# Score products in row-half tile order, and new engine orders, in a four-layer attention and GLU kernel

## The chip, the cores and the metric

The kernel runs on one core of a Trainium2 chip. The metric is the device time of one execution in microseconds (us). The time before is 384.71 us, the median of three runs (384.37 to 385.68).

## The reference

The input `x` has 2048 tokens of 448 values in bf16. It goes through four layers; each layer normalizes its rows (mean and variance) and adds its result to `x`:

```python
x = x + _A_ref(_layernorm(x), wqkv, wo)
x = x + _B_ref(_layernorm(x), w_gate, w_up, w_down)
x = x + _A_ref(_layernorm(x), wqkv, wo)
x = x + _B_ref(_layernorm(x), w_gate, w_up, w_down)
```

`_A_ref` is attention with 16 heads of 28 values. Token s looks at 8 tokens only: s, s-2, s-4, ... s-14. Its logits are scaled, the missing tokens at the start are masked, a softmax follows, then the sum of the values and the product with `wo`. `_B_ref` is `(x @ w_gate) * (x @ w_up) @ w_down` with an inner width of 1792. Both attention layers share their weights, and so do both GLU layers.

## The kernel before, in words

Layers 0 and 2 are attention, layers 1 and 3 are the GLU. Tokens are put in two halves, even and odd ones, so that the window of 8 tokens at distance 2 becomes 8 neighbours. `x_sb` holds 16 blocks of 128 tokens. Each layer goes in chunks of 256 or 512 tokens (`ACH`, `BCH`, `SEQ`); chunks of neighbouring layers run beside each other.

**The long products.** TensorE does nearly all of its work in a mode where the array is split in two row halves of 64 rows and 128 columns (`MAIN = "R64"`). Two products, one per half, run at once: a *pair*. Queries and keys (`qk_chunk`), values (`v_group`), the gate and up products (`b_chunk`), the down product and the product with `wo` (`y_blocks`, both by `twin_blocks`) are all such pairs, issued through `whole` in the helper `pair` (profile line 347). A pair streams 256, 336, 448 or 512 columns.

**The short products.** Attention itself works on query blocks of 120 tokens (`qb_info`), two at a time. `attn_front` makes the scores: 32 products per query block, each with a key tile of 64 rows by 32 columns and some 64 to 80 query columns (line 831, mode `BURST = "C32"`). In the first eleven query blocks of layer 0 (`WIDE_S`) the tiles are 64 by 64 and there are 16 per block (mode C64). ScalarE takes the exponential (line 841), VectorE applies the mask (848), and `attn_back` multiplies with the values: 32 products per query block, on tiles of 64 by 32 (line 866). The result is copied out (880), its two parts are added (884), and `norm` divides by the sum (894 to 907). Their tiles sit at eight positions of the array: two row halves by four column strips. Which position follows which in time is set by the list comprehension on line 826 for scores and on line 859 for values. For values the column strip is the inner index: four strips of one row half, then four of the other. For scores before the change the row half `p` is the inner index: it alternates with every product.

**Bursts.** Short products and long products need different modes, so a run of short products stands between long ones as a *burst*. A burst can also be *merged*: some pairs of a long product next to it (its host) are then issued as eight products of 32 columns each, one per tile position (`strip`, line 350), in the same mode as the short ones, and the short products are put between these *sets of strips* in portions of eight. A set of strips does the work of one pair.

**The order of the work.** Every operation is an `Op` with its dependencies. The order on each engine is written out in the table `ORDER` (line 101), and the PSUM banks of each product in `BANKS` (163); `schedule` and `emit` only turn them into waits. An entry `A+B*H/k/f` in TensorE's list is a merged burst: the first f pairs of host H as they are, then the short products of A and B with k sets of strips of H between them, then the rest of H. Copies from PSUM (`QK` line 708, `V` line 800, `Oc` line 880, the transposes' 623) may be on ScalarE or VectorE; the lists say which. SyncE's list holds the loads, the transposing DMAs of the normalized rows (line 602) and the stores.

**The GLU's chain.** Rows of `x` after an attention layer are added by VectorE (924), get their statistics (578, 580) and are normalized (599), all on VectorE with two small steps on ScalarE; a transposing DMA then brings them to `xnTb`, and only then can the gate products of that chunk begin.

Of the kernel before, what the change touches and what calls it, by code (L numbers as in the profile page):

```python
# [93 lines left out]
def grp_nc(g):  # L94
# [22 lines left out]
    ),  # L117
    "act": (
# [12 lines left out]
    ),  # L131
    "dve": (
# [18 lines left out]
    ),  # L151
    "pool": (
        "21 24 39 28 23 18 29 35 40 25 36 26 20 32 44 33 37 19 27 22 41 34 38 42 30 65 43 31 63"
# [222 lines left out]
def build(nc, A_x, A_wqkv, A_wo, B_w_gate, B_w_up, B_w_down, out):  # L376
# [433 lines left out]
    def attn_front(li, g, prio):  # L810
        qbs, nc = grp_qbs(g), grp_nc(g)
        nd = len(qbs)
# [11 lines left out]
        KN = 64 if wide else 32  # L824
# [281 lines left out]
```

## Time and profile before

| | us |
|---|---|
| median of three runs | 384.71 |
| the profiled execution | 384.78 |
| its span (first to last instruction) | 382.8 |
| TensorE busy | 377.2 |
| VectorE busy | 288.7 |
| ScalarE busy | 197.2 |

The span is what the trace shows; the 1.98 us between it and the execution's time lie around it. A row of the timeline reads: start, length from the first start to the last end, engine, line, operation, tiles, shape, and the number of instructions that were merged into the row. The end of a product is modelled, so the start of the next row is the better mark. A row of the windows names a stretch and then each engine's busy time in it with the number of its instructions.

### The profile page before, as it was taken

What the parts mean: (1) busy time and instruction counts of PE and PEld (TensorE: products, weight loads), DVE (VectorE), ACT (ScalarE), POOL (GpSimd) and SP (SyncE); (2) the same over time, 40 slices, a digit from 0 to 9 for tenths busy, and PEclk for the clock granted to TensorE, in tenths of its full rate; (3) what the DMA queues carried; (4) which work ended last, traced back from release to release, by engine and by line L of the source; (5) the groups of instructions that cost most, each with busy time, mean ns of one, the idle gap of its engine ahead of it and who ended that gap; (6) DMA issues with size and microseconds to landing.
All of it is one profiled execution on the core that took longest, in us unless ns stands there. A gap on an engine that the chain in (4) does not pass through costs nothing.

```text
span 382.8 us, 14279 instructions
## 1 busy us (share of the span) xinstructions
PE 377.2 (99%) x6338; PEld 210.8 (55%) x6338; DVE 288.7 (75%) x652; ACT 197.2 (52%) x383; POOL 7.1 (2%) x33
## 2 busy tenths in 40 slices
PE   8999999999999999999999999999999999999997
PEld 3655577544454545446766666555555444445665
DVE  7998999998756876897567888668899687174443
ACT  4897887566426356156456236448653534125220
POOL 6000000000000000000000000000000000000000
PEclk9999999999999999999999999999999999999999
DMA  7665542700421030232001214320124002313004
GB/s 251 171 161 135 122 116 65 105 3 2 81 39 39 11 56 19 50 62 47 6 15 38 50 29 76 73 36 8 35 46 75 2 3 60 64 23 38 2 2 134
DMA packets 54880, 22.49 MB, mean 59 GB/s; under 512 B 45012, under 2 KB 54820, under 8 KB 54820
## 3 DMA queue, kind: packets, MB, share of 16 engines
q1 hardware_dynamic: 54676, 21.53, 26.5%
q8 instruction: 50, 0.82, 0.9%
q14 instruction: 10, 0.08, 0.1%
q10 hardware_dynamic: 144, 0.06, 0.1%
HBM read 8.54 MB, written 2.71 MB: 29 GB/s over the span
## 4 chain that ended last, share of the span: by engine, by line
PE 89%; DVE 6%; DMA 1%; ACT 1%; issue 1%; SPq 0%; DVEq 0%
PE ps L347 81%; PE ps L350 3%; PE ps L831 2%; PE ps L866 2%; PE ps L975 1%; DVE st L578 1%; DMA xnTb<-xn_sb 1%; DVE xn_sb L599 1%; DVE E_sb L848 1%; DVE x_sb L924 1%; DMA x_sb<-in_A_x_dram 1%; DVE oT L907 0%; PE ps L613 0%; DVE hT L963 0%; DVE R_sb L894 0%
## 5 line engine op out<-in xcount | busy, mean ns | idle before, releaser
L347 PE MATMUL ps<-xnTb,WGU 64*128 64x512 bf16 (+1 forms) x1900 | 173.7, 332 | 0.3
L347 PEld LDWEIGHTS ps<-xnTb,WGU 64*128 64x128 bf16 x1900 | 92.4, 94 | 71.5 <-ACT g_sb L960 1.5
L960 ACT ACTIVATE g_sb<-ps 128x512 bf16<-128x512 f32 (+1 forms) x140 | 69.0, 509 | 112.4 <-PE ps L347 93.8
L963 DVE TENSOR_TENSOR hT<-g_sb,ps 128x512 bf16<-128x512 bf16 (+1 forms) x140 | 77.7, 573 | 43.2 <-ACT g_sb L960 41.8
L347 PE MATMUL ps<-WD,hT 64*128 64x448 bf16 x802 | 83.5, 349 | 0.1
L347 PEld LDWEIGHTS ps<-WD,hT 64*128 64x128 bf16 x802 | 38.5, 94 | 33.4 <-DVE hT L963 0.5
L347 PE MATMUL ps<-xnTa,WQK 64*128 64x512 bf16 (+1 forms) x486 | 52.7, 352 | 0.6 <-issue 0.3
L924 DVE TENSOR_TENSOR x_sb<-x_sb,ps 128x448 bf16<-128x448 bf16 x62 | 36.8, 611 | 18.2 <-PE ps L347 18.1
L841 ACT ACTIVATE E_sb<-ps,shift_sb 128x1024 bf16<-128x1024 f32 (+1 forms) x36 | 37.5, 1068 | 11.6 <-PE ps L831 11.4
L578 DVE BATCH_NORM_STATS2 st<-x_sb 128x6 f32<-128x448 bf16 x64 | 38.5, 615 | 1.5 <-DMA x_sb<-in_A_x_dram 1.3
L599 DVE TENSOR_SCALAR xn_sb<-x_sb,mv,rstd 128x512 bf16<-128x512 bf16 (+1 forms) x64 | 35.1, 567 | 4.7 <-ACT rstd L583 4.5
L347 PEld LDWEIGHTS ps<-xnTa,WQK 64*128 64x128 bf16 x486 | 23.4, 94 | 18.4 <-issue 0.4
L708 ACT ACTIVATE qk<-ps 128x1024 bf16<-128x1024 f32 (+1 forms) x28 | 25.7, 929 | 8.7 <-PE ps L347 6.1
L347 PE MATMUL ps<-wo_g,oT 64*128 64x448 bf16 x256 | 29.5, 350 | 0.1
L895 ACT ACTIVATE R_sb<-R_sb 128x480 f32<-128x480 f32 (+1 forms) x34 | 19.9, 601 | 15.7 <-DVE R_sb L894 15.6
L848 DVE TENSOR_TENSOR E_sb<-E_sb,MK 128x1024 bf16<-128x1024 bf16 (+1 forms) x36 | 23.1, 656 | 5.2 <-ACT E_sb L841 5.2
L907 DVE TENSOR_TENSOR oT<-O_sb,R_sb 128x480 bf16<-128x480 f32 (+3 forms) x36 | 21.8, 624 | 6.5 <-ACT R_sb L896 6.5
L347 PE MATMUL ps<-WV,xnTa 64*128 64x336 bf16 (+3 forms) x252 | 23.3, 304 | 0.0
L894 DVE STREAM_SHUFFLE R_sb<-O_sb 128x480 f32<-128x480 f32 (+1 forms) x34 | 22.8, 691 | 0.0
L896 ACT ACTIVATE R_sb<-R_sb 128x480 f32<-128x480 f32 (+1 forms) x34 | 19.9, 599 | 0.2
L347 PEld LDWEIGHTS ps<-wo_g,oT 64*128 64x128 bf16 x256 | 12.1, 94 | 11.1 <-DVE oT L907 0.7
L866 PEld LDWEIGHTS ps<-E_sb,v_sb 64*32 64x32 bf16 x1088 | 12.6, 90 | 8.2 <-issue 3.6
(61 smaller groups left out, 215.4 us busy)
## 6 DMA issues: line engine op xcount, KB each, us to landing
out_dram<-x_sb SPq DMA_DIRECT2D x15, 112.0 KB, 1.8
x_sb<-in_A_x_dram SPq DMA_DIRECT2D x3, 448.0 KB, 5.7
hT<-in_A_wqkv_dram SPq DMA_DIRECT2D x4, 224.0 KB, 4.8
WGU<-in_B_w_gate_dram SPq DMA_DIRECT2D x4, 224.0 KB, 4.0
WGU<-in_B_w_up_dram SPq DMA_DIRECT2D x4, 224.0 KB, 4.4
WD<-in_B_w_down_dram SPq DMA_DIRECT2D x2, 448.0 KB, 4.9
WGU<-in_B_w_gate_dram SPq DMA_DIRECT2D x2, 336.0 KB, 4.6
WGU<-in_B_w_up_dram SPq DMA_DIRECT2D x2, 336.0 KB, 4.4
```

The costliest lines, as they stand in the source:

```text
L347: return lambda E: E.matmul(out(), lhs(), rhs(), start=start, stop=stop)
L578: sc.add("dve", one(lambda E, B=B: E.bn_stats(st6[:, B, :], x_sb[:, B, :]), ("bn", li, B)), 525.0, deps=[("x", li - 1, B)] + ([("xn", li - ...
L599: sc.add("dve", one(lambda E, B=B, dst=dst, src=src: E.tensor_scalar(dst, src, mv[:, B, 0:1], rstd[:, B:B + 1], ALU.subtract, ALU.mult), ( ...
L708: return E.activation(dst, src, ACT.Copy) if hasattr(E, "activation") else E.tensor_copy(dst, src)
L841: return E.activation(E_sb[:, slot, 2 * hp:2 * hp + 2, 0:w], ps[:, b0:b0 + 2, 0:w], ACT.Exp, bias=shift_sb[:, 0:1], scale=SCALE)
L848: return E.tensor_tensor(e, e, MK[:, kind, 0:nc].unsqueeze(1).unsqueeze(1).to_broadcast([128, 2, w // nc, nc]), ALU.min)
L866: parts[eb // 2].append((lambda E, b=b, c=c, o=o, vw=vw, eb=eb, eo=eo: E.matmul(ps[32 * b:32 * b + 32, bk[c], o:o + nc], vw, E_sb[64 * c:6 ...
L894: sc.add("dve", one(lambda E: E.stream_shuffle(R_sb[:, rs, 0:w], O_sb[:, os_, 0:w], [DH] * 32), ("Rs", li, qb)), dve_est(w) + 20.0, deps=[ ...
L907: return E.tensor_tensor(oT[:, :, a % HALF:a % HALF + z - a], O[:, :, a - tok:z - tok], R_sb[:, rs, 0:w].rearrange("p (h n) -> p h n", h=4 ...
L924: sc.add("dve", one(lambda E: E.tensor_tensor(x_sb[:, B, :], x_sb[:, B, :], ps[:, bk[w], 0:D], ALU.add), ("x", li, B)), dve_est(D), deps=[ ...
L960: sc.add("act", one(lambda E, gs=gs, bk=bk: E.activation(g_sb[:, gs, 0:nt], ps[:, bk[0], 0:nt], ACT.Copy), ("G", li, j, fc)), act_est(nt), ...
L963: sc.add("dve", one(lambda E, gs=gs, bk=bk, fc=fc: E.tensor_tensor(hT[:, fc, hs, 0:nt], g_sb[:, gs, 0:nt], ps[:, bk[1], 0:nt], ALU.mult), ...
```

## The change

One line of the code changes, that of the scores' order, and the tables `ORDER` and `BANKS` are new from end to end.

```diff
-        for hc, d, c, s_, p in [(hc, d, c, s_, p) for hc in range(4) for d in range(nd) for c in range(2) for s_ in range(64 // KN) for p in range(2)]:
+        for hc, d, p, c, s_ in [(hc, d, p, c, s_) for hc in range(4) for d in range(nd) for p in range(2) for c in range(2) for s_ in range(64 // KN)]:
```

The scores now go through four column strips of one row half and then through four of the other, as the values and the strips do. Of the tables, these entries of TensorE's list show the kind of difference (two of the list's pieces, in order):

```diff
-525 530 347 542 531 543 350 602 351 603 560*352/1/6 353 428
+542+560+543*353/6/1 428 602 429 603
...
-1325 1204 1326 1205 1365+1347+1348*1258/7 1261 1267 1278 1366 1270 1279 1335 1280 1371+1372*1271/7 1336
+1365*1204/1/3 1366*1205/1 1267 1325 1278 1326 1279 1270 1271 1280 1281 1347+1348+1371+1372*1272/7 1273 1335
```

Here 560, 1365 and 1366 are scores of one query block each; 542, 543, 1347, 1348, 1371 and 1372 are values. Counted through both lists, the bursts are:

| kind of burst | before | after |
|---|---|---|
| 32 short products of 32-column tiles, alone (one of those before has one set of strips) | 20 | 7 |
| 64 of them, without strips | 1 | 3 |
| 64 of them, one set of strips | 0 | 1 |
| 64 of them, two sets | 7 (6 scores, 1 values) | 14 (7 scores, 5 values, 2 mixed) |
| 64 of them, three to seven sets | 7 (all values) | 0 |
| 96 of them | 1 (seven sets) | 2 (five and six sets) |
| 128 of them | 1 (five sets) | 2 (seven sets each) |
| 16 products of 64-column tiles, alone | 4 | 2 |
| 32 of them, together | 3 | 4 |
| the first scores of layer 0 | 1 | 1 |

TensorE's list has 6338 products before and 6314 after, since 58 sets of strips become 54. VectorE's list grows from 595 to 600 entries and ScalarE's shrinks from 383 to 378: 19 copies move from ScalarE to VectorE and 14 the other way. In SyncE's list the four transposing DMAs of layer 1's second chunk stand at places 63, 64, 67 and 68 before, and at 61, 63, 64 and 65 after. At the start, all of the warming products stand before the first long product; at the end the order of the last three down products is 448, 224, 224 columns before and 224, 448, 224 after, the last of them the same.

128 rows, old and new, of tables (BANKS, ORDER) are left out of this document.

## The prediction

> **What bounds the kernel now.** I read the page's busy times first, then the windows, then the timeline of TensorE alone.
>
> ```profile
> PE 377.2 (99%) x6338; PEld 210.8 (55%) x6338; DVE 288.7 (75%) x652; ACT 197.2 (52%) x383; POOL 7.1 (2%) x33
> ```
>
> TensorE (PE) is busy for 377.2 of 382.8 us. A busy TensorE is not one at its peak, so the question is what stands in that time beside long products. The windows say who else is near its limit:
>
> ```profile
> 50.00:100.00 50.00, 49.78 (x984) 28.27 (x980) 47.04 (x109) 35.16 (x73) 0.00 (x0) 1.00 0.31 60
> 100.00:150.00 50.00, 50.00 (x848) 25.10 (x846) 34.41 (x73) 23.77 (x43) 0.00 (x0) 1.00 0.23 41
> ```
>
> The third busy time is VectorE's (DVE). From 50 to 100 us it has 47.04 of 50 us, so both engines bind there; from 100 us on it has 34.41, and TensorE alone sets the pace. The granted clock is 1.00. So a microsecond that leaves TensorE's list is worth a microsecond after 100 us and perhaps half of one before.
>
> What the long products cost when nothing disturbs them, from their own rows:
>
> ```profile
> 369.13 2.46 PE L347 MATMUL ps<-xnTb,WGU 64*128 64x256 bf16 x42
> 371.42 1.49 PE L347 MATMUL ps<-WD,hT 64*128 64x448 bf16 x14
> 372.75 0.93 PE L347 MATMUL ps<-xnTb,WGU 64*128 64x256 bf16 x14
> ```
>
> Start to start, 21 pairs of 256 columns take 2.29 us, 0.109 a pair; seven pairs of 448 take 1.33, 0.190 a pair. Now the burst's price can be read. It is the start of the next long row, less the start of the long row before plus that row's pairs, less one pair for each set of strips, since a set does a pair's work.
>
> ```profile
> 198.66 1.30 PE L347 MATMUL ps<-WD,hT 64*128 64x448 bf16 x12
> 199.89 0.32 PE L866 MATMUL ps<-E_sb,v_sb 64*32 64x64 bf16 x32
> 200.14 0.94 PE L347 MATMUL ps<-xnTb,WGU 64*128 64x256 bf16 x14
> 201.01 0.34 PE L866 MATMUL ps<-E_sb,v_sb 64*32 64x64 bf16 x32
> 201.28 1.12 PE L347 MATMUL ps<-WD,hT 64*128 64x448 bf16 x10
> 202.33 0.29 PE L831 MATMUL ps<-Qz,qk 64*32 64x64 bf16 x24
> ...
> 203.17 0.74 PE L347 MATMUL ps<-WD,hT 64*128 64x448 bf16 x6
> ```
>
> A lone burst of 32: 198.66 + 6 x 0.190 = 199.80, and the next long row starts at 200.14: 0.34 us. The one after: 200.14 + 7 x 0.109 = 200.90, against 201.28: 0.38. I use 0.36. A merged burst of 64 scores with two sets: 201.28 + 5 x 0.190 = 202.23, next 203.17, less two pairs: 0.56, where two lone bursts would be 0.72. Changing over and back is most of a lone burst, and that is what merging saves.
>
> **The change part by part.** I count the bursts in both lists (the table above) and price each kind. The other prices come from these rows:
>
> ```profile
> 276.33 0.92 PE L347 MATMUL ps<-wo_g,oT 64*128 64x448 bf16 x8
> ...
> 279.36 3.20 PE L347 MATMUL ps<-xnTb,WGU 64*128 64x512 bf16 x28
> 282.38 1.50 PE L347 MATMUL ps<-WD,hT 64*128 64x448 bf16 x14
> 283.83 0.59 PE L831 MATMUL ps<-Qz,qk 64*32 64x64 bf16 x32
> 284.35 0.93 PE L347 MATMUL ps<-WD,hT 64*128 64x448 bf16 x8
> ```
>
> A pair of 512 columns is (282.38 - 279.36)/14 = 0.216. The 96 short products with seven sets that stand in the gap: 276.33 + 0.76 = 277.09 to 279.36 is 2.27, less 7 x 0.216: 0.76. The lone scores at 283.83 should cost 0.36, but 282.38 + 1.33 = 283.71 to 284.35 is 0.64: 0.28 of it is a stall.
>
> ```profile
> 252.15 0.92 PE L347 MATMUL ps<-WD,hT 64*128 64x448 bf16 x8
> ...
> 254.94 1.12 PE L347 MATMUL ps<-WD,hT 64*128 64x448 bf16 x10
> ```
>
> 128 short products with five sets: 252.91 to 254.94 is 2.03, less 5 x 0.190: 1.08.
>
> ```profile
> 287.81 1.11 PE L347 MATMUL ps<-WD,hT 64*128 64x448 bf16 x10
> ...
> 290.54 0.74 PE L347 MATMUL ps<-WV,xnTa 64*128 64x336 bf16 x8
> ```
>
> 64 values with seven sets: 288.76 to 290.54 is 1.78, less 1.33: 0.45. Thirty-two more short products thus cost 0.09 over a lone burst, if enough sets stand between them.
>
> ```profile
> 42.90 0.92 PE L347 MATMUL ps<-WV,xnTa 64*128 64x448 bf16 x8
> 43.75 0.71 PE L866 MATMUL ps<-E_sb,v_sb 64*32 64x64 bf16 x64
> 44.40 0.61 PE L347 MATMUL ps<-xnTa,WQK 64*128 64x256 bf16 x8
> 44.94 0.80 PE L831 MATMUL ps<-Qz,qk 64*64 64x128 bf16 x32
> 45.92 0.50 PE L347 MATMUL ps<-xnTa,WQK 64*128 64x256 bf16 x6 [0.18 <-DVE qk L708]
> ```
>
> 64 without strips: 43.66 to 44.40, 0.74, as much as two lone bursts, so joining alone gains nothing. The scores of 64 by 64 tiles behind it: 44.84 to 45.92, 1.08, with a wait for VectorE's copy in it.
>
> ```profile
> 36.55 0.93 PE L347 MATMUL ps<-wo_g,oT 64*128 64x448 bf16 x8
> 37.41 0.42 PE L831 MATMUL ps<-Qz,qk 64*64 64x128 bf16 x16
> 37.76 0.93 PE L347 MATMUL ps<-wo_g,oT 64*128 64x448 bf16 x8
> ```
>
> ```profile
> 58.48 0.72 PE L347 MATMUL ps<-xnTb,WGU 64*128 64x256 bf16 x10
> 59.13 0.64 PE L831 MATMUL ps<-Qz,qk 64*64 64x128 bf16 x32
> 59.71 1.70 PE L347 MATMUL ps<-xnTb,WGU 64*128 64x256 bf16 x28
> ```
>
> Sixteen of them alone: 37.31 to 37.76, 0.45. Thirty-two together, undisturbed: 59.03 to 59.71, 0.68.
>
> Before: 20 x 0.36 = 7.20; 0.74; seven with two sets, 3.92; seven with more sets at 0.48 (between 0.45 and 0.56, nearer the first), 3.36; 0.76; 1.08; 4 x 0.45 = 1.80; 3 x 0.68 = 2.04. Sum 20.90.
>
> After: 7 x 0.36 = 2.52; 3 x 0.74 = 2.22; the one with one set 0.65 (between 0.56 and 0.74); seven scores with two sets 3.92, seven others at 0.52 (between 0.45 and 0.56) 3.64; two of 96 at 0.65 (between 0.45 + 0.09 and 0.76), 1.30; two of 128 at 0.80 (between 0.45 + 0.18 and 1.08), 1.60; 0.90; 4 x 0.68 = 2.72. Sum 19.47. **The burst term is -1.43 us.** With all unknown prices at their low ends it is -2.57, at their high ends -0.28.
>
> **Stalls.** Two stalls of before sit in bursts: 0.28 at 283.83 and 1.08 - 0.68 = 0.40 at 44.94. The new lists put both scores elsewhere; a moved wait can come back under another name, so I take half, -0.34 (0 to -0.68).
>
> **The scores' own order.** In the rows above 24 scores in alternating order have 0.29 from first start to last end, 32 values in the new order 0.32. Eight products more for 0.03 is the pace of either, so I take nothing; one portion of eight either way in each of some 17 bursts is 17 x 0.03 = 0.5, and I keep both signs for the range. The rival of the weight loads is below.
>
> **Cover.** From 50 to 100 us the lists have, by the same prices, 3.00 us of bursts before that differ (the seven lone ones of 32 from the fifth query block's values to the thirteenth's scores, 2.52, and one of 64 at 0.48) and 0.74 + 0.65 + 0.52 + 0.52 = 2.43 after. VectorE has only 2.96 us to spare there. I give back half of the difference, +0.28, as TensorE will wait for VectorE in part.
>
> **Moved copies and the ends.** Five copies more on VectorE lie, beyond 100 us, beside 15.59 us of idle time in that row of 50, and cost nothing; if that cover failed they would cost a wait each. The warming products at the start stand beside VectorE's first normalizations, which TensorE waits for anyway; at the end the last product, its addition and its store are unchanged. Nothing for both. SyncE's transposing DMAs of layer 1's second chunk are issued two to three places earlier in its list, past loads of values that now follow; those are needed later in TensorE's list too.
>
> Sum: -1.43 - 0.34 + 0 + 0.28 = -1.49. The profiled execution took 384.78 us (span 382.8 and 1.98 around it), the median of the runs 384.71, so no correction is needed: 384.78 - 1.49 = **383.3 us**.
>
> **The rivals.** *A late normalization (slower).* The place is the start of the second GLU chunk:
>
> ```profile
> 73.08 3.61 DMA xnTb<-xn_sb
> 76.73 6.65 PE ps L347 x60
> ```
>
> The chain of waits runs there through VectorE's normalization and a transposing DMA of 3.61 us, not through TensorE. If the new VectorE list reaches the last normalization of that chunk late, TensorE stands still and every microsecond counts, as VectorE cannot catch up with 2.96 us to spare. It is slower than before from a wait of 1.5 us more; if one DMA falls wholly behind instead of beside the work, the wait is 3.61, less the 1.49: 386.9. Against it: in VectorE's list the four normalizations stand at places 151, 153, 160 and 161 before and 145, 147, 159 and 160 after, and their DMAs move forward on SyncE. For it: every other chunk of the GLU has such a chain, and all were placed anew.
>
> *The big bursts wait (no change).* A burst of 128 values needs the results of four query blocks and fills four banks; the one burst of 128 in the trace costs 1.08 where 0.63 would do. If every merged burst comes at its high end and both stalls come back elsewhere, -0.28 is left: 384.5.
>
> *All merges at their low price (faster still).* -2.57 and both stalls gone, -0.68, no cover lost: 381.5.
>
> *Weight loads (slower).* If loads into one row half could not run beside products of that half, each 32 scores would come at the unprefetched pace: in the joined burst at 43.75 the second 32 cost 0.74 - 0.36 = 0.38 more. 23 query blocks have 32 such scores each (six in layer 0, seventeen in layer 2), and 23 x 0.38 = 8.7 us: 392.0. The values are in that order already and pay 0.34 to 0.38 a burst, so I give it 0.02. [...]
>
> *The change does nothing of this* only if the lists were not what runs; they are the program's order, so 0.01.
>
> **How the numbers follow.** A measurement of this kernel can tell about 0.3%, 1.15 us, from no change: faster is below 383.56, slower above 385.86. The forecast has 0.50 (its own range 382.3 to 384.2; 0.35 of it counts as faster, 0.15 as the same), all merges low 0.18 (faster), the big bursts 0.13 (same), the late normalization 0.16 (slower 0.14, same 0.02), the loads 0.02 (slower), nothing 0.01 (same). Faster 0.53, same 0.31, slower 0.16. The range of 381.2 to 386.0 takes in the low prices with a little of the order's own 0.5, and the milder part of the late normalization.
>
> **What would show it.** Right: TensorE's rows show 96 and 128 short products between long rows at 0.65 and 0.80, the pairs of lone value bursts at 200 us gone, and 24 scores still at 0.29. Wrong: a new wait of TensorE for xnTb or for a copy of over 0.5 us, above all between 60 and 100 us; scores slower than 0.03 for eight; bursts of 128 above 1.1; or VectorE busy below 45 of the 50 us from 50 to 100, which would mean that it, too, was kept waiting.

## The result, and the profile after

The changed kernel takes **382.75 us** (median of four runs, 382.69 to 383.0), the kernel before beside it 385.19 (384.37 to 385.9): a ratio of 0.9939, with an interval of 0.9915 to 0.9962. The forecast was 383.3 with a range of 381.2 to 386.0. Two runs among the experiments, in which the granted clock fell to 0.66 and 0.76 as a mean of the whole run, are left out of all figures.

The kernel before scatters more than the changed one: over all its runs here it took 383.8 to 386.1 us (one run 387.9), and what its higher runs have is not shown, since its profile is from the lower part. So the gain is read below from the two profiles, 384.78 and 382.75 us, and not from the 2.44 us between the medians.

The profiled execution has a span of 380.9 us, where before had 382.8. First the busy times and the windows of the changed kernel; a window's row has the stretch and then PE, PEld, DVE, ACT and POOL:

```profile
PE 375.1 (98%) x6314; PEld 209.7 (55%) x6314; DVE 292.1 (77%) x657; ACT 195.2 (51%) x378; POOL 7.5 (2%) x33
```

```profile
0.00:50.00 50.00, 46.57 (x852) 25.85 (x853) 45.79 (x130) 39.77 (x74) 7.48 (x33) 1.00 0.61 162
50.00:100.00 50.00, 50.00 (x1092) 29.57 (x1064) 47.11 (x108) 33.52 (x68) 0.00 (x0) 1.00 0.28 56
100.00:150.00 50.00, 50.00 (x734) 24.79 (x732) 36.09 (x77) 23.60 (x46) 0.00 (x0) 1.00 0.34 51
```

TensorE's busy time fell by 2.1 us, about as much as the span (1.9). From 50 to 100 us TensorE has no idle time in this row now, beside a VectorE that is busy for 47.11 us, as before (47.04).

The timeline of TensorE in the changed kernel answers the prediction's prices and shows the one new wait that counts:

```profile
44.85 0.64 PE L831 MATMUL ps<-Qz,qk 64*64 64x128 bf16 x32 [0.16 <-ACT O_sb L880]
...
47.85 0.74 PE L347 MATMUL ps<-WV,xnTa 64*128 64x336 bf16 x8
48.95 0.94 PE L347 MATMUL ps<-xnTb,WGU 64*128 64x256 bf16 x14 [0.36 <-ACT E_sb L841]
...
147.87 1.31 PE L347 MATMUL ps<-WD,hT 64*128 64x448 bf16 x12
...
149.95 1.50 PE L347 MATMUL ps<-WD,hT 64*128 64x448 bf16 x14
151.28 1.03 PE L347 MATMUL ps<-xnTb,WGU 64*128 64x512 bf16 x8
...
162.56 1.49 PE L347 MATMUL ps<-WD,hT 64*128 64x448 bf16 x14
...
165.60 1.69 PE L347 MATMUL ps<-xnTb,WGU 64*128 64x512 bf16 x14
...
254.00 1.68 PE L347 MATMUL ps<-xnTa,WQK 64*128 64x512 bf16 x14
...
257.81 1.25 PE L347 MATMUL ps<-xnTb,WGU 64*128 64x512 bf16 x10
```

Read them as the prediction did, from one long row to the next. A burst of 128 with seven sets: 254.00 + 7 x 0.216 = 255.51, next 257.81, less seven pairs of 512 columns: 0.79. One of 96 with five sets: 162.56 + 7 x 0.190 = 163.89, next 165.60, less 5 x 0.216: 0.63. One of 64 with one set: 147.87 + 6 x 0.190 = 149.01, next 149.95, less one pair: 0.75. And a wait: four pairs of 336 columns (0.143 each, between the 0.109 of 256 and the 0.190 of 448) end at 48.42, and the gate product of the second layer begins at 48.95, 0.53 later, held by the exponential of the scores just issued (ScalarE, line 841), whose bank it needs.

All bursts priced in this way:

| kind of burst | forecast | measured after |
|---|---|---|
| lone 32 | 0.36 | 0.34 to 0.37 |
| 64 without strips | 0.74 | 0.72 to 0.74 |
| 64, one set | 0.65 | 0.75 |
| 64, two sets, scores | 0.56 | 0.52 to 0.58 |
| 64, two sets, values or mixed | 0.52 | 0.51 to 0.60 |
| scores 13 and 14, two sets in two hosts | 0.56 | 0.67 |
| 96 | 0.65 | 0.73 and 0.63 |
| 128 | 0.80 | 0.79 and 0.83 |
| 16 wide | 0.45 | 0.45 twice |
| 32 wide | 0.68 | 0.67 three times, 0.98 with a wait in it |
| sum, with stalls | 19.81 | 19.88 |

The sum leaves out the first scores. Before had 21.62 by the same count, so bursts and the stalls inside them gave 1.74 us. The first scores themselves gave nothing. These are the rows around them, of before and then of the changed kernel:

```profile
20.93 0.41 PE L613 MATMUL ps<-ident,xn_sb 64*128 64x64 bf16 x16
21.28 0.31 PE L831 MATMUL ps<-Qz,qk 64*64 64x144 bf16 x8
...
22.39 0.82 PE L347 MATMUL ps<-xnTa,WQK 64*128 64x512 bf16 x6
```

```profile
20.77 0.30 PE L613 MATMUL ps<-ident,xn_sb 64*128 64x64 bf16 x8
21.00 0.51 PE L831 MATMUL ps<-Qz,qk 64*64 64x144 bf16 x16
21.97 0.29 PE L613 MATMUL ps<-ident,xn_sb 64*128 64x64 bf16 x8 [0.46 <-DVE xnTa L623]
22.23 0.82 PE L347 MATMUL ps<-xnTa,WQK 64*128 64x512 bf16 x6
```

Both times 16 transposing products (line 613) and the 16 first scores stand between two long rows and take 1.46 us; the new list only puts eight of the transposes behind the scores. The long row behind them begins 0.16 sooner (22.23 against 22.39). The waits between long products behind that point stayed the same in all, 1.03 before and 1.06 after. So -1.74 - 0.16 + 0.03 = -1.87, against -1.9 of the spans.

### The profile page after: what moved, and what is told of

It is laid out like the page before. It is cut to its first block, busy times and chain, and to the rows that moved or that the text cites. A ratio compares the mean times of both kernels' runs of the same rounds, so it can differ in the third digit from the quotient of the medians.

```text
span 380.9 us, 14241 instructions
## 1 busy us (share of the span) xinstructions
PE 375.1 (98%) x6314; PEld 209.7 (55%) x6314; DVE 292.1 (77%) x657; ACT 195.2 (51%) x378; POOL 7.5 (2%) x33
## 4 chain that ended last, share of the span: by engine, by line
PE 94%; ACT 3%; DMA 1%; SPq 1%; DVE 0%; issue 0%
PE ps L347 86%; PE ps L350 3%; PE ps L831 2%; PE ps L866 2%; PE ps L975 1%; ACT E_sb L841 1%; DMA WV<-in_A_wqkv_dram 1%; ACT qk L708 1%; SPq L440 1%; PE ps L613 1%; ACT v_sb L800 0%; ACT xnTa L623 0%; DVE WQK L525 0%; ACT O_sb L880 0%; DVE x_sb L979 0%
## 5 line engine op out<-in xcount | busy, mean ns | idle before, releaser
L347 PE MATMUL ps<-xnTb,WGU 64*128 64x512 bf16 (+1 forms) x1922 | 175.7, 333 | 0.4 <-ACT E_sb L841 0.4
L347 PE MATMUL ps<-WD,hT 64*128 64x448 bf16 x796 | 80.7, 349 | 0.0
L924 DVE TENSOR_TENSOR x_sb<-x_sb,ps 128x448 bf16<-128x448 bf16 x62 | 37.0, 614 | 20.9 <-PE ps L347 20.3
L347 PE MATMUL ps<-xnTa,WQK 64*128 64x512 bf16 (+1 forms) x490 | 51.5, 352 | 0.2 <-issue 0.2
L708 ACT ACTIVATE qk<-ps 128x1024 bf16<-128x1024 f32 (+1 forms) x27 | 24.1, 909 | 12.3 <-PE ps L347 8.9
L347 PE MATMUL ps<-wo_g,oT 64*128 64x448 bf16 x244 | 28.4, 350 | 0.0
L581 ACT ACTIVATE lnv<-mv,eps_sb 128x2 f32<-128x2 f32 (+1 forms) x33 | 9.5, 292 | 16.2 <-DVE mv L580 16.1
```

What stands on the lines that cost most here:

```text
L347: return lambda E: E.matmul(out(), lhs(), rhs(), start=start, stop=stop)
L708: return E.activation(dst, src, ACT.Copy) if hasattr(E, "activation") else E.tensor_copy(dst, src)
L924: sc.add("dve", one(lambda E: E.tensor_tensor(x_sb[:, B, :], x_sb[:, B, :], ps[:, bk[w], 0:D], ALU.add), ("x", li, B)), dve_est(D), deps=[ ...
```

## The experiments

### Merging undone: how much do the merged bursts carry?

All merged bursts are taken apart, so that short products and their host stand behind each other; the rest of the lists is unchanged.

```diff
-561+566*461/2/3
+461 561 566
```

> The changed kernel with every merged burst undone: the short products stand together, the host whole before or behind them. Theory (a burst without strips pays 0.38 for each 32 products after the first 32): fourteen bursts of 64 go from 0.54 to 0.74, two of 96 from 0.68 to 1.12, two of 128 from 0.81 to 1.50, together 5.0 us: 387.8. Rival (the gain came from fewer waits, not from the bursts): not over 384.

Measured: **387.96 us** (387.59 to 388.5), ratio to before 1.0091 (1.0078 to 1.0105). This is TensorE's timeline around the last burst of 128:

```profile
289.75 2.62 PE L347 MATMUL ps<-WD,hT 64*128 64x448 bf16 x26
292.31 1.48 PE L866 MATMUL ps<-E_sb,v_sb 64*32 64x64 bf16 x128
293.71 2.82 PE L347 MATMUL ps<-WD,hT 64*128 64x448 bf16 x28
```

289.75 + 13 x 0.190 = 292.22 and the next long row starts at 293.71: 128 products cost 1.49 without strips between them and 0.83 with seven sets. Summed over all bursts, 25.5 against 20.9 with the first scores, 4.6 of the 5.2 us. The merged bursts are what the kernel gains by; joining bursts alone would have given nothing, as the prediction said of the row at 43.75. This kernel also shows what a burst's price is made of. Without strips 32 short products cost 0.34 to 0.39, 64 nearly always 0.72, 96 cost 1.02 and 1.13, and 128 cost 1.31 and 1.49: about 0.36 for each 32, however many stand together, so no fixed price for changing over and back is left to see. Merging makes the short products themselves cheaper; by what mechanism, no run here shows.

### The scores' order alone: before with the new order, after with the old

```diff
-        for hc, d, c, s_, p in [(hc, d, c, s_, p) for hc in range(4) for d in range(nd) for c in range(2) for s_ in range(64 // KN) for p in range(2)]:
+        for hc, d, p, c, s_ in [(hc, d, p, c, s_) for hc in range(4) for d in range(nd) for p in range(2) for c in range(2) for s_ in range(64 // KN)]:
```

This line in the kernel before:

> The kernel before with the scores' new order alone. Theory (the order of tile positions inside a burst is worth nothing, both are at the pace of about 0.03 us for eight): 384.8 (384.5 to 385.1), the same as before. Rival (row halves in turn let the loads run beside products, so alternating is better): slower, over 385.5. Rival (the new order saves some 0.03 us in each of some 23 blocks): 384.1.

Measured: **384.44 us** (384.23 to 385.67, twelve runs), before 384.38; ratio 1.0001 (0.9984 to 1.0017). That interval alone would still let the rival's half a microsecond through (0.13%); the traces settle it, for the bursts sum to 21.6 us in the kernel before with either order (20.94 and 20.91 without the burst at 25 us). The order is worth nothing, and the rival of the weight loads falls with it.

The reverse, the changed kernel with the old line:

> The changed kernel with the scores' line of before (row half alternating), lists as after. Theory (the gain is the bursts'; tile order is worth nothing): 382.8 within 0.3, the 24 scores ahead of the first set of strips again at 0.29 us. Rival 1 (the scores' order brings part of the gain): 383.3 or more, half a microsecond lost over 23 query blocks. Rival 2 (weight loads into one row half hold each other up, so that alternating is better): below 382.4.

Measured: 383.15 us (382.3 to 385.33, twelve runs), ratio 0.9972 (0.9957 to 0.9987). That decided nothing: the twelve runs fall in two groups, seven from 382.3 to 383.2 and five from 384.0 to 385.3. The changed kernel itself, run again beside it without any edit,

> The changed kernel once more, beside the runs that follow. Theory (fewer and better filled bursts): 382.8 us within 0.2, and the bursts in its trace sum to about 20.9 us against 23.1 before. Rival (the gain is a good day of the chip): over 384.

gave 382.77 us (ratio 0.9955, 0.9942 to 0.9967) in six runs, of which five lie from 382.36 to 383.08, and the profiled one at **385.39**. So there was a second effect, in some executions of one and the same program.

### What the upper group has: TensorE without instructions

The waits of TensorE in the repeated run's profile (what waited, for what; us in all, times, longest) name it first:

```profile
PE ps L350 <- issue: 1.4, 1, 1.4
```

"Issue" means that the engine waited for nothing that the profile shows. Its timeline has the place, in the middle of the burst of 128:

```profile
257.91 0.29 PE L866 MATMUL ps<-E_sb,v_sb 64*32 64x64 bf16 x16
259.56 0.41 PE L350 MATMUL ps<-xnTa,WQK 64*32 64x512 bf16 x8 [1.37 <-issue]
```

In the first profile of the same kernel this burst ran without a gap. The gap is the largest part of the 2.7 us by which this execution's span is longer: the burst gives 1.6, the first scores begin 0.9 later (21.86 against 21.00), and waits give 0.3. The profile of the kernel with the old line, from its upper group too (384.11), names the same wait at the same place, and its span is 1.4 us longer than that of the first profile:

```profile
PE ps L350 <- issue: 1.1, 1, 1.1
```

What differs is the queue that the profile names instruction. This is its row among the DMA queues of the repeated run, in the whole span, and then from 256.9 to 258.1 us (packets, MB, share):

```profile
q8 instruction: 50, 0.82, 0.9%
...
q8 instruction: 1, 0.02, 5.1%
```

Fifty packets for 2 x 6314 loads and products are 253 instructions each, with the semaphore instructions 255; 0.82 MB / 50 is 16.4 kB. I take 256 for a packet, an estimate next to this 255. Counted so from the first instruction, the gap stands at 35.75 packets, and the packet landed at 258.0 us, where the gap begins. The packet began to move at 257.0, 0.2 us behind the start of the burst. In the undisturbed profile of the same kernel its row from 242.0 to 252.9 us has two packets, and none follows until the burst is nearly over:

```profile
q8 instruction: 2, 0.03, 1.4%
```

There the second of them started at 252.0, 3.6 us ahead of the burst. So I formed the theory that a burst with strips can use up 256 instructions sooner than the next packet comes.

**More sets** use up instructions faster: a pair is 4 instructions, a set is 16. Fifteen entries were given twice their sets:

```diff
-561+566*461/2/3
+561+566*461/4/2
```

> The changed kernel with four sets of strips in place of two in its merged bursts of 64 (two in place of one in the two bursts of 32 that stand next to each other), the first set up to two pairs earlier. Theory (the price falls with the sets, as 0.45 at seven sets and 0.54 at two says): fourteen times 0.07, about 0.9 us less: 381.9. Rival (the bursts begin earlier and wait for the masks or exponentials): 382.8 or more.

Measured: **385.73 us** (385.06 to 386.42), ratio 1.0032 (1.0019 to 1.0046). The theory of the price alone fell, though the price did what it should; a burst of values that nothing disturbs:

```profile
96.72 1.67 PE L347 MATMUL ps<-xnTb,WGU 64*128 64x512 bf16 x14
...
99.56 0.61 PE L347 MATMUL ps<-xnTb,WGU 64*128 64x512 bf16 x4
```

96.72 + 7 x 0.216 = 98.23, next 99.56, less four pairs: 0.46, where two sets cost 0.51. But TensorE's waits have new lines:

```profile
PE ps L866 <- issue: 1.4, 1, 1.4
PE ps L347 <- issue: 1.3, 3, 0.7
PE ps L347 <- ACT E_sb L841: 0.5, 1, 0.5
PE ps L866 <- DVE E_sb L848: 0.3, 1, 0.3
```

The three longest gaps without a semaphore stand at 27.75, 36.75 and 44.75 packets of 256. Always three quarters, as at 35.75: that points to the packets' edges, and it bears out the 256, since with 255 to a packet the first and the last of these would lie 17 instructions apart in their packets. The last two lines are waits for results, of which the first was there before (0.36 at 48.95).

**Moving the edges** tells cause from company. Some of the warming products at the start are cut into narrow pieces, which shifts the whole stream behind them by 40 or by 168 instructions and leaves everything else as it is (lines of these kernels are numbered one to three higher):

```diff
+PIECES = {5: 5, 6: 5, 7: 5, 8: 5, 9: 5}
...
-        sc.add("pe", one(lambda E, n=n: E.matmul(ps[:, n % NBK if n < NBK else wb[0], :], warm[:, 0:128], warm, start=True, stop=True), ("warm", n)), 427.0 if n < WARM else 216.0, deps=["c_warm"], mode="F",
+        k = PIECES.get(n, 1)
+        m, g = (128, 512) if k == 1 else (32, 96)
+        sc.add("pe", [((lambda E, n=n, m=m, g=g: E.matmul(ps[0:m, n % NBK if n < NBK else wb[0], 0:g], warm[:, 0:m], warm[:, 0:g], start=True, stop=True)), ("warm", n) if i == k - 1 else None) for i in range(k)], 427.0 if n < WARM else 216.0, deps=["c_warm"], mode="F",
```

> The changed kernel; five of the warming products at the start are cut into five narrow pieces each, so that TensorE's instruction stream behind them lies 40 instructions (20 loads, 20 products) further on; everything else is unchanged. Theory of the instruction supply: TensorE's instructions come in 50 packets of the queue named instruction, 256 instructions each; the stretch that TensorE stood still for 1.4 us without a semaphore inside the burst of 128 (TensorE time 258.0 in the repeated run of the changed kernel) lies exactly at the edge of a packet, and the packet's worth of instructions before that edge took only 3.2 us. Moved by 40, no packet's worth is consumed in under 4.3 us, so the standstill is gone in the profile and in every run: median 382.5 (382.2 to 382.8), no run above 383.5. Rival (the standstill comes from transposing DMAs or by chance, and not from the place in the stream): as the changed kernel, 382.8, with about one run in six at 384 to 385.4.

Measured: **382.64 us**, eleven runs from 382.33 to 383.01; ratio 0.9947 (0.9929 to 0.9964). No run is in the upper group, and the profile names no wait for "issue" within bursts.

> The changed kernel with 84 narrow warming products more at the start (nine warming products in pieces), so that the stream behind them lies 168 instructions further on. Theory of the instruction supply: edges of packets now fall so that four packets' worth are consumed in 1.56, 1.58, 1.47 and 1.35 us (ends at about 72.8, 165.6, 257.4 and 290.4 us of the changed kernel's trace); a new packet is there about 3.6 us after the one before, so TensorE stands still for about 2.0, 2.0, 2.1 and 2.2 us at these four places, with no semaphore named: 382.8 + 8.3 = 391 (388 to 393). Rival (place in the stream does not matter): 382.8, and at most 1 us for a longer start, which the first row of long products shows.

Measured: **392.53 us** (389.96 to 393.3), ratio 1.019 (1.0148 to 1.0233), with not one line of the attention or the GLU changed. TensorE's waits, its timeline at two of the four places, and the windows behind the last:

```profile
PE ps L869 <- issue: 5.1, 3, 2.1
PE ps L834 <- issue: 0.9, 2, 0.6
```

```profile
262.70 0.21 PE L869 MATMUL ps<-E_sb,v_sb 64*32 64x64 bf16 x4 [1.50 <-issue]
...
297.96 0.21 PE L869 MATMUL ps<-E_sb,v_sb 64*32 64x64 bf16 x4 [2.10 <-issue]
```

```profile
293.00:298.00 5.00, 2.90 (x176) 2.06 (x174) 2.46 (x5) 0.00 (x0) 0.00 (x0) 1.00 0.41 79
298.00:303.00 5.00, 5.00 (x60) 2.34 (x62) 3.28 (x9) 1.28 (x3) 0.00 (x0) 0.66 0.02 3
303.00:308.00 5.00, 5.00 (x124) 2.66 (x120) 3.78 (x8) 4.51 (x8) 0.00 (x0) 1.00 0.15 49
```

All four places that the count of instructions named have a gap at an edge (11.75, 23.75, 36.75 and 41.75 packets): 1.7, 0.7, 1.7 and 2.3 us between starts, where 2.0, 2.0, 2.1 and 2.2 were expected. The expectation took 3.6 us from one packet to the next; from edge to edge it was 3.2, 2.3, 3.2 and 3.6 here. Two smaller ones (0.8 and 0.6) were not foreseen; one of them lies at an edge, 28.75, the other at 21.36 does not and stays open. They sum to 7.7. Most of the rest of the 9.3 us by which the span is longer comes after the longest gap: the granted clock was 0.66 as a mean of the next five us, 1.7 us lost. The mean clock of the whole run was 0.996 in this and two more of the four runs; in the fourth it was 1.00, and that run took 389.96.

The packets' own times show the link. Taken in order, one packet to an edge, every gap at an edge of over 0.5 us between starts in these traces (one each in the repeated run, the old order and the kernel with the same tile four times below, three with four sets, five here) ended 2.2 to 2.8 us after its packet had begun to move, 1.3 to 1.6 us after it had landed, and at no edge of any trace did TensorE go on sooner than 2.2 us after the packet's start. At the edge in the burst of 128 the packet began 2.5 us before TensorE went on in the repeated run, and 4.8 us before in the first profile, which has no gap. So a late packet is what TensorE stood for, and the instruction supply is shown as the cause of the gap that sets the upper group apart; why the same packet comes nearly 4 us later in one execution than in another is not. In the late case transposing DMAs moved data until about a microsecond before it, but no run here separates that.

The order of the scores could now be asked again without that effect, the old line and the shift by 40:

> The changed kernel with the old order of the scores and with the stream moved by 40 instructions. With the old order alone, half of the runs were at 382.3 to 383.2 and half at 384.0 to 385.3. Theory (the tile order is worth nothing; the upper half was the standstill at the packet's edge): the upper half is gone, median 382.7 (382.4 to 383.0), no run above 383.5, the same as the new order moved by 40. Rival (the new order itself saves about half a microsecond): 383.2, and both halves are still there.

Measured: **382.54 us** (382.1 to 383.24, six runs), ratio 0.994 (0.9918 to 0.9962): the upper group is gone, and old and new order (382.54 and 382.64) agree.

### The same tile four times in a row

```diff
-        for hc, d, p, c, s_ in [(hc, d, p, c, s_) for hc in range(4) for d in range(nd) for p in range(2) for c in range(2) for s_ in range(64 // KN)]:
+        for d, p, c, s_, hc in [(d, p, c, s_, hc) for d in range(nd) for p in range(2) for c in range(2) for s_ in range(64 // KN) for hc in range(4)]:
```

> The changed kernel with the scores of four heads in a row on the same tile position, in place of changing tiles at every product. If a product has to wait until the one before has left its tile, 64 columns take about 0.027 us at the pace of the long rows (448 columns in 0.190), where a product in a burst takes about 0.0083 + 0.003: each block of 32 scores costs some 0.5 us more, and 29 blocks some 14: 395 to 402. If the order of tiles matters nothing whatever it is: 382.8.

Measured: 385.69 us, one run. Neither. Its waits have a gap of 1.36 us for "issue" in the burst of 128, at 35.75 packets, which is the effect above. Without it the span is some 1.5 us longer than that of the changed kernel. The timeline of this kernel, and then of the changed one, at the 64 scores without strips:

```profile
239.37 0.81 PE L831 MATMUL ps<-Qz,qk 64*32 64x64 bf16 x64
```

```profile
238.47 0.70 PE L831 MATMUL ps<-Qz,qk 64*32 64x64 bf16 x64
```

0.11 for two blocks, 0.05 a block. So a row of products on one tile costs something, a tenth of the 0.5 estimated for full serialization, and the two orders tried that change tiles with every product cost the same.

### Does VectorE bind from 50 to 100 us?

```diff
-                e = E_sb[:, slot, 2 * hp:2 * hp + 2, 0:w].rearrange("p b (m n) -> p b m n", n=nc)
+                w_ = nc if li == 0 else w
+                e = E_sb[:, slot, 2 * hp:2 * hp + 2, 0:w_].rearrange("p b (m n) -> p b m n", n=nc)
```

> The changed kernel with the mask of layer 0 applied only to the first group of columns of each bank, so that most of layer 0's mask is left out (its scores outside of the window count in the softmax) and VectorE has some 8 us less to do between 20 and 110 us. The prediction's term of cover says that TensorE waits for VectorE there when bursts get cheaper. Theory (from 50 to 100 us VectorE does not bind, the new waits lie in the first 50 us behind DMAs and ScalarE): within 0.4 us of the changed kernel, 382.4 to 382.8. Rival (VectorE binds there): what the chain through VectorE holds up, 0.5 to 2 us, is given back: 381 to 382.

Measured: 383.67 us (382.17 to 384.28, ten runs), ratio 0.9961 (0.9944 to 0.9978). By the time it is undecided, since the runs scatter over 2 us. The profiled one, the fastest, has no gap in the burst of 128, so its trace can be compared with the first of the changed kernel. Windows of this kernel, and two rows of its timeline:

```profile
0.00:50.00 50.00, 46.97 (x888) 26.16 (x890) 43.25 (x131) 40.23 (x75) 7.54 (x33) 1.00 0.64 162
50.00:100.00 50.00, 50.00 (x1034) 29.30 (x1032) 44.08 (x108) 33.20 (x68) 0.00 (x0) 1.00 0.28 56
```

```profile
20.57 0.51 PE L831 MATMUL ps<-Qz,qk 64*64 64x144 bf16 x16
...
48.36 0.94 PE L347 MATMUL ps<-xnTb,WGU 64*128 64x256 bf16 x14
```

VectorE lost 3.0 us of work from 50 to 100 us and 2.5 before that. The span is 0.5 shorter, but the first scores already start 0.43 sooner (20.57 against 21.00), and the gate product 0.59 sooner (48.36 against 48.95). Behind 50 us nothing more is gained: VectorE, busy for 47 of 50 us, did not hold TensorE.

### Looking for a better version

First, more sets wherever the count of instructions allows it, with the stream shifted by 40. Some of the entries:

```diff
-643+644*689/2
+643+644*689/4
-799*724/1/6 800
+799+800*724/4/3
-1167+1191+1168+1192*1307/3/1+1313/4
+1167+1191+1168+1192*1307/2/1+1313/3
```

(two sets fewer in the last, and scores 1 and 2 of layer 2 joined.)

> The changed kernel with four sets of strips in place of two in eight merged bursts, three in two, the lone scores at the third query block of layer 2 joined to the burst before, one set fewer in the burst of 128, and the stream moved by 40 instructions, chosen so that hardly a packet's worth of instructions is consumed in under 3.4 us. By the prices measured in the run with four sets everywhere (0.05 to 0.07 less for a burst, 0.25 for a joined one): 382.8 - 1.0 = 381.7 (381.2 to 382.3), with no standstill of over 0.5 us without a semaphore. Rival (more sets cost TensorE time by themselves): 384 or more, nearer to the 385.7 of four sets everywhere.

Measured: **385.98 us** (385.64 to 386.96, eleven runs), ratio 1.0038 (1.0021 to 1.0055). TensorE's waits in it:

```profile
PE ps L348 <- ACT qk L711: 0.9, 1, 0.9
PE ps L834 <- DVE Qz L822: 0.5, 1, 0.5
PE ps L348 <- ACT E_sb L844: 0.4, 1, 0.4
```

No long gap for "issue" is left, as the count wanted; in its place are waits for results. The second line explains itself: with `/4/3` in place of `/1/6` the scores start three pairs, 0.57 us, sooner, before their masked queries are there. The list was tight to some tenths of a microsecond at such places.

So two bursts were moved later instead of sooner, to hosts behind them:

```diff
-799*724/1/6 800 725
+724 799+800*725/4
...
-1365*1204/1/3 1366*1205/1
+1204 1365+1366*1205/3
```

> The changed kernel with two bursts moved one long product later in TensorE's list, so that four and three sets of strips stand between their short products in place of one and two: the scores of query blocks 1 and 2 of layer 2 (0.74 in the changed kernel's trace, at 149 us) and those of 13 and 14 (0.67, at 277 us). The moves put 36 instructions more ahead of the burst of 128 at 255 us, so that an edge of packets now falls into its middle and the packet's worth around it takes over 4 us in place of 3.2. Theory (price of a burst, instruction supply): 0.50 and 0.52, so 0.24 + 0.15 less: 382.75 - 0.39 = 382.4 (382.1 to 382.7), no run above 383.5. Rival (results that come later are waited for at once, as in the runs with more sets): 383 to 384.5, with a wait for a result of VectorE or ScalarE behind one of the two bursts.

Measured: **382.74 us** (382.47 to 383.0, six runs), ratio 0.9944 (0.9925 to 0.9963): the same as the changed kernel, and no run in the upper group. This is a second way of moving the stream: with the shift by 40 (either order of the scores) and with this one, none of 23 runs is above 383.3, where 6 of 22 runs of the changed kernel and its twin with the old line are. Its timeline at the first of the two:

```profile
147.79 1.50 PE L347 MATMUL ps<-WD,hT 64*128 64x448 bf16 x14
...
150.39 0.74 PE L347 MATMUL ps<-WD,hT 64*128 64x448 bf16 x6
151.29 1.90 PE L347 MATMUL ps<-xnTb,WGU 64*128 64x512 bf16 x16 [0.17 <-ACT E_sb L841]
```

147.79 + 7 x 0.190 = 149.12, next 150.39, less four pairs: 0.51, as forecast (0.75 in the changed kernel). But the gate product then starts at 151.29, where it started at 151.28 before: it needs the bank that the exponential of these scores frees. The gain turned into a wait at once. The second burst gained little to begin with:

```profile
276.02 0.92 PE L347 MATMUL ps<-wo_g,oT 64*128 64x448 bf16 x8
...
277.96 0.36 PE L347 MATMUL ps<-wo_g,oT 64*128 64x448 bf16 x2
```

276.02 + 4 x 0.190 = 276.78, next 277.96, less three pairs: 0.61, where 0.52 was expected and the changed kernel has 0.67.

No version beats the changed kernel's usual 382.75 by what can be measured. The shift by 40 takes away its upper group.

## Why the prediction was right, point by point

**The bursts: right in size, wrong in the reason given.** Forecast -1.43 and -0.34 for stalls, measured -1.74 together. Single prices missed by up to 0.11, the larger ones mostly because the burst cost more than forecast: one set of strips is worth nothing (0.75 against 0.74 with none), a burst of 96 cost 0.73 and 0.63. The undone merging confirms that this is the source. But the prediction said that changing over and back is most of a lone burst and that merging saves that. Its own row at 43.75 (64 products at 0.74, two lone bursts' worth) and the undone merging (about 0.36 for each 32, up to 128 together) show no such fixed part. The forecast did not suffer, since every price came from a row and not from that reason.

**The stalls: right in size.** The 0.28 at 283.83 is gone. Of the 0.40 in the wide scores of blocks 5 and 6, 0.30 is still there (the row at 44.85, 0.98 - 0.68), and it waits for a copy on ScalarE now, as it did for one on VectorE. Taking half was a guess, and it came out by one stall going and the other staying.

**The scores' order: right,** nothing (1.0001, and 382.54 against 382.64).

**Cover: wrong, the largest miss.** The prediction gave back 0.28 since VectorE would hold TensorE from 50 to 100 us. All waits behind the first scores grew by 0.03. Those in that stretch went from 0.63 to 0.08, and those before 50 us from 0.22 to 0.86; the largest, 0.53 at 48.95, is a wait for ScalarE's exponential, which holds a bank. The kernel with a smaller mask shows that 3 us less on VectorE bring nothing behind 50 us. The step that failed is the inference from a share of busy time to a bound.

**Nothing at the two ends: missed by 0.16.** The long row behind the first scores begins that much sooner. This is within scatter: with the same instructions ahead of them, the first scores began at 21.00, 21.86 and 20.94 us in three profiles (the changed kernel twice, once with the old scores). Cover and this start are the difference between -1.49 and -1.9; they lie on the same side, so nothing cancelled there.

**The rivals.** No late normalization: the wait at the second GLU chunk (0.6 us of the weight loads for xnTb before) is gone. The loads into one row half cost nothing that shows (384.44 against 384.38); that the second 32 at 43.75 cost 0.38 because their loads came late, as this rival had it, no run shows, since 32 alone cost 0.34 to 0.39 too. "The big bursts wait" came true in part, though not by its mechanism: the burst of 128 does stand still in some executions, but for instructions and not for four query blocks' results, and the gap was then 1.3 to 1.6 us between starts. None of the rivals had that. Of the signs named for being right, bursts of 96 and 128 came at 0.63 to 0.83, and 24 scores (23 in one row of the timeline) still take 0.29; of those for being wrong, a new wait of over 0.5 us did come, but at 48.95 and for an exponential.

## What to carry to other kernels

Where an engine is busy throughout, price what stands between its long rows, each kind from rows of its own, and count the kinds; the sum of 35 small prices came out within 0.1 us, though single ones missed by as much, and though the reason given for them was wrong. Do not turn a neighbour's high busy share into a bound without a wait that names it. When one program's runs fall into two groups, look for gaps named "issue", count the instructions up to them, and shift the stream by a few cheap instructions: if the gaps follow, it is the supply.

## What the runs showed of the hardware

- TensorE's instructions came in 50 packets of 16.4 kB, 255 to each by the count. With 256 to a packet, my estimate, eleven gaps in five profiles stand at the same three quarters of a packet, from 11.75 to 44.75: 0.6 to 2.3 us between starts. TensorE went on 2.2 to 2.8 us after the packet had begun to move and 1.3 to 1.6 us after it had landed. Most of these packets' worth had been used up in 1.4 to 3.8 us, two in some 5. At one and the same edge the packet began 4.8 us before TensorE went on in the profile without a gap, and 2.5 us before in the one with a gap of 1.4. The changed kernel took 382.64 us with its stream moved by 40 instructions and 392.53 with it moved by 168.
- After a gap of 2.1 us (and a row of PE busy for 2.90 of 5 us) the granted clock was 0.66 in the next five us. In four profiles whose longest gap was 1.1 to 1.4 us it was 1.00 as a mean of the whole run.
- Short products on tiles of 64 by 32 cost about 0.36 us for each 32 when they stand together, from 32 to 128 of them; with two sets of strips between them 64 cost 0.51 to 0.60, with seven sets 128 cost 0.79 and 0.83.
- Small products in a row on the same tile cost 0.05 us a block of 32 more than products that change tiles each time; between alternating row halves and going through one half first no difference shows (ratio 1.0001, 0.9984 to 1.0017).
